# A token mixer on one core: wo's low parts go to VectorE, and VectorE's order in an iteration changes

## The chip, the cores and the metric

The kernel runs on one core of a Trainium2 chip. Its time is the device time of one execution in microseconds, the median over several executions. One core has five engines with a queue each: TensorE (PE, with its weight loads listed as PEld), VectorE (DVE), ScalarE (ACT), GpSimd (POOL) and SyncE (SP, which here only issues DMAs). An engine runs its instructions strictly in their order, so one that waits holds up all behind it.

## The reference

The input is x with 2048 tokens of 512 channels, in float32. The kernel computes

```
h  = x + attention(layernorm(x)) @ wo      # 32 heads of 16; features softmax(k@phi), softmax(-k@phi)
                                           # num = phi_q (phi_k^T v), den = phi_q (sum phi_k), o = num/den
h2 = h + mlp(layernorm(h))                 # over tokens: gelu(h^T w1 + b1) w2 + b2, 1792 hidden
```

The attention is linear: the sums over the keys (kv and zacc) are made first, and then each tile of queries is multiplied with them.

## The kernel before

Tokens are worked in 16 tiles of 128 (tile t). To keep float32 accuracy, every operand of a large product is split into a high part, which ACT makes by a copy into a rounded type, and a low part, which is the difference; a product is three matmuls (`mm3`, L61 to L63): high by high, high by low, low by high. All names ending in h and l, or in hi and lo, are such pairs.

There are four stages.

1. To about 120 us: keys and values of all tiles and the first queries, with sums of the keys' features in zacc (on POOL, L197 and L472).
2. A short passage to about 148 us (L471 to L509). The last tile's features are added to zacc by DVE (L481); PE multiplies zacc with ones, in two halves of four groups each (L486, tile pk_ps); ACT copies the result to zB, and POOL multiplies it with the queries' features (s_ez, L440, tile ez). wo is split here: `wo_hi` on ACT, `wo_lo` on POOL (L429, tile wol), two of its four parts before POOL's negate and two behind the first two ez.
3. Iterations 0 to 18 of the loop at L620, to about 276 us. In iteration `it` PE runs s_num(it-1) (L544), s_wo(it-2) (the product with wo, tile po), s_tr(it) (transposes, L526, tile tn), a query projection q_mm while there are any, and then fills: parts of the next stage's first product, `h^T w1`, for hidden groups p=0 and p=1 (tile pu).
4. The rest of the mixer: fills of the other groups, gelu, and the product with w2 (L745), with all operands split.

From L416 to the end of stage 3 the order of PE, DVE, ACT and POOL is written out by hand (`manual_schedule`): an engine executes what the Python code issues, in that order. In stage 1 and in stage 4 a scheduler sets the order.

In an iteration of stage 3 the steps that matter are these.

- s_num writes its result to the PSUM tile tn. ACT copies it to oh (L548), and DVE makes the low part ol from tn and oh (`s_ol`, L553). s_tr writes the same PSUM tile, of which there is one, so it waits until ol is made.
- `q_logits` is DVE's mx, mn and a shift (L151, L152, L144) with an ACT copy (L146, tile eq) of the other sign. That copy frees one of two PSUM slots of the query projections. The first fill of p=1 takes these slots when the projections are over, in iteration 5. POOL's `negate` (L159) then follows, and ACT's exponential.
- `q_sums` is two reductions (L214). `s_den` is DVE's chain from ez to w (L449 to L455, tile tz first), interleaved one by one with the lists above by `run`.
- `lead` puts POOL's eq by w (`s_pq`, L458) and ez (L440) for later tiles.
- `s_h(it-2)` adds the product with wo to x (L568), which frees po, of which there is one too, for the next s_wo. It stores h and then makes the mean and variance (L571 to L575, here called the statistics). `s_rstd` on POOL (L578, L579, tile r) uses these in the next iteration, `s_hn` on ACT normalizes and splits, and POOL makes the low part hs (L57).
- `fill_load` loads a piece of w1 by SP (L595, tile wraw) into one of four buffers, and splits it: ACT makes whi (L56), DVE makes wlo (L57). It stands at the end of an iteration, behind the statistics. Iterations 2, 6 and every second one after load two pieces, iterations 4 and 5 one each.

Of the kernel before, what the change touches and what calls it, by code (L numbers as in the profile page):

```python
# [11 lines left out]
AF = mybir.ActivationFunctionType  # L12
# [7 lines left out]
NT = S // P  # L20
KD = D // P
# [12 lines left out]
def block_kernel(ctx: ExitStack, tc: tile.TileContext, x, xT, wT, phic, wo, w1, b1, w2, b2,  # L34
                 kvmask, ident_in, out):
    nc = tc.nc
# [17 lines left out]
    def split(hi, lo, src, lo_engine):  # L54

        nc.scalar.activation(hi, src, AF.Copy)  # L56
        return lo_engine.tensor_sub(lo, src, hi)  # L57

    def mm3(o, ah, al, bh, bl, first, last):

        nc.tensor.matmul(o, ah, bh, start=first, stop=False)  # L61
        nc.tensor.matmul(o, ah, bl, start=False, stop=False)  # L62
        nc.tensor.matmul(o, al, bh, start=False, stop=last)  # L63
# [24 lines left out]
    zacc = wp.tile([P, NG, P], F32, name="zacc")  # L88
# [5 lines left out]
    X, XH, EQ, PK, VS, SQ, PS, W = {}, {}, {}, {}, {}, {}, {}, {}  # L94

    def load_x(t):
        raw = kk.tile([P, KD, P], F32, name="xraw", bufs=3)
        nc.sync.dma_start(raw, xT[t])
        return raw
# [36 lines left out]
    def logit_ops(src, e, pool):  # L136

        v = src.rearrange("p (j h d) -> p j h d", h=2, d=DH)
        ev = signs(e)
        mx = wk.tile([P, NPR, 2], F32, name="mx")  # L140
        mn = wk.tile([P, NPR, 2], F32, name="mn")

        def shift():
            nc.vector.tensor_sub(ev[:, :, 0], v, mx.unsqueeze(3).to_broadcast([P, NPR, 2, DH]))  # L144
            if pool:
                nc.scalar.activation(ev[:, :, 1], v, AF.Copy)  # L146
                MN.append((ev, mn))
            else:
                nc.vector.tensor_sub(ev[:, :, 1], mn.unsqueeze(3).to_broadcast([P, NPR, 2, DH]), v)

        return [lambda: nc.vector.tensor_reduce(mx, v, axis=AX.X, op=ALU.max),  # L151
                lambda: nc.vector.tensor_reduce(mn, v, axis=AX.X, op=ALU.min),  # L152
                shift]

    def negate():

        if MN:
            ev, mn = MN.pop(0)
            nc.gpsimd.tensor_sub(ev[:, :, 1], mn.unsqueeze(3).to_broadcast([P, NPR, 2, DH]), ev[:, :, 1])  # L159

    def run(*lists):

        for i in range(max(map(len, lists))):
            for ops in lists:
                if i < len(ops):
                    ops[i]()

    def exps(t, e):
        nc.scalar.activation(e, e, AF.Exp, scale=r1[:, t:t + 1])
# [39 lines left out]
    def q_sum(t):  # L209

        assert t < SUMS or t - SUMS in W, "a tile's sums would go where others are still wanted"
        SQ[t] = sums[:, t % SUMS]
        e = signs(EQ[t])
        return [lambda c=c: nc.vector.reduce_sum(SQ[t][:, :, 1 - c], e[:, :, c], axis=AX.X) for c in range(2)]  # L214
# [144 lines left out]
    def q_mm():  # L359
        if q["mm"] < NT:  # L360
            PS[q["mm"]] = proj(q["mm"], wqh, wql, ps_q, "pu")
            q["mm"] += 1

    def q_logits(lag):
        n = q["logits"]
        if n < min(NT, q["mm"] - lag + NT * (q["mm"] == NT)):
            EQ[n] = big.tile([P, NG, P], F32, name="eq", tag="big")
            q["logits"] += 1
            return logit_ops(PS[n], EQ[n], n >= len(Q_AT))
        return []  # L370
# [7 lines left out]
    def q_sums(lag):  # L378
        n = q["sum"]
        if n < min(NT, q["exp"] - lag + NT * (q["exp"] == NT)):  # L380
            q["sum"] += 1
            return q_sum(n)
        return []

    def v_kv():

        nonlocal v
        v_proj(v)
        if v % 2 == 0:
            kv(v - 2)  # L390
            kv(v - 1)
        v += 1
# [4 lines left out]
    for t in range(3, NT - 1):  # L397
        if t + 2 < NT:
            raw = load_x(t + 2)
# [22 lines left out]
    woh = w2p.tile([P, KD, D], F32R, name="woh")  # L422
    wol = w2p.tile([P, KD, D], F32R, name="wol")

    def wo_hi(j):
        nc.scalar.activation(woh[:, j], WO[j], AF.Copy)

    def wo_lo(j):
        nc.gpsimd.tensor_sub(wol[:, j], WO[j], woh[:, j])  # L429

    WO = {}
    for j in range(KD):
# [5 lines left out]
    def s_ez(t):  # L438
        EZ[t] = az.tile([P, NG, P], F32, name="ez")
        nc.gpsimd.tensor_mul(EZ[t], EQ[t], zB)  # L440
# [33 lines left out]
    k_norm(NT - 1, False)  # L474
    for j in range(KD):
        wo_hi(j)
    wo_lo(0)
    wo_lo(1)
    v_kv()
    run(q_logits(0))  # L480
    nc.vector.tensor_add(zacc, zacc, PK[NT - 1])  # L481
    negate()
    zB = big.tile([P, NG, P], F32, name="zB", tag="big")
    for g in range(2):
# [3 lines left out]
    q_exp(0)  # L488
    s_ez(0)
    s_ez(1)  # L490
    wo_lo(2)
    wo_lo(3)
    q_mm()
    v_kv()
    run(s_den(0))
# [24 lines left out]
    HN, HT, PHT, OS, PO, VE = {}, {}, {}, {}, {}, {}  # L520
# [16 lines left out]
    def s_num(t):  # L537

        pn = ps_t.tile([P, 2, 4, P], F32, name="tn")[:, :, 0:2]
        for b in range(2):  # L540
            for c in range(4):
                for r in range(2):
                    rows, cols = slice(64 * r, 64 * r + 64), slice(32 * c, 32 * c + 32)
                    nc.tensor.matmul(pn[cols, r, b, :], kvB[rows, b, cols], PHT[t][rows, 4 * b + c, :],  # L544
                                     start=True, stop=True, skip_group_check=True)
        oh = ak.tile([P, 2, 2, P], F32R, name="oh")
        ol = ak.tile([P, 2, 2, P], F32R, name="ol")
        nc.scalar.activation(oh, pn, AF.Copy)  # L548
        OS[t] = oh, ol, pn

    def s_ol(t):
        oh, ol, pn = OS[t]
        return [lambda: nc.vector.tensor_sub(ol, pn, oh)]  # L553
# [7 lines left out]
    def s_x(t):  # L561
        HT[t] = ak.tile([P, D], F32, name="h", bufs=4)
        nc.sync.dma_start(HT[t], x[t * P:(t + 1) * P, :])

    def s_h(t):

        h = HT[t]
        nc.vector.tensor_add(h, PO.pop(t), h)  # L568
        nc.sync.dma_start(out[t * P:(t + 1) * P, :], h)
        st = ak.tile([P, 6], F32, name="st2")  # L570
        nc.vector.bn_stats(st, h)  # L571
        nc.vector.bn_aggr(mv2[:, t, :], st)
        VE[t] = ak.tile([P, 2], F32, name="ve2")
        nc.vector.tensor_scalar(VE[t][:, 0:1], mv2[:, t, 1:2], 1.0 + EPS, EPS * EPS, op0=ALU.mult, op1=ALU.add)
        nc.vector.tensor_scalar_mul(VE[t][:, 1:2], mv2[:, t, 0:1], -1.0)  # L575

    def s_rstd(t):
        nc.gpsimd.tensor_tensor(r2[:, t:t + 1], VE[t][:, 0:1], mhalf[:, :1], op=ALU.pow)  # L578
        nc.gpsimd.tensor_mul(VE[t][:, 1:2], VE[t][:, 1:2], r2[:, t:t + 1])  # L579
# [7 lines left out]
    w1v = w1.rearrange("(k p) f -> p k f", p=P)  # L587
    w2v = w2.rearrange("(k p) s -> p k s", p=P)

    def stream(src, k0, n, c0, w):  # L590

        raw = wf.tile([P, n, w], F32, name="wraw")
        wh_ = wf.tile([P, n, w], F32R, name="whi")
        wl_ = wf.tile([P, n, w], F32R, name="wlo")
        nc.sync.dma_start(raw, src[:, k0:k0 + n, c0:c0 + w])  # L595
        LO.append(split(wh_, wl_, raw, nc.vector).ins)
        return wh_, wl_

    PU, WI, LO = {}, {}, []
    FN, FL = [0] * (NF // 2), [0] * (NF // 2)  # L600

    def fill_load(p):
        if FL[p] < NT:
            WI[p, FL[p]] = stream(w1v, FL[p], 2, p * 256, 256)
            FL[p] += 2

    def fill(p, pool=None):

        t = FN[p]
        FN[p] = t + 1  # L610
        if FL[p] <= t:
            fill_load(p)
        if t == 0:
            PU[p] = [pool.tile([P, D], F32, name="pu", tag="pu") for _ in range(2)]
        a, b = WI[p, t - t % 2]
        for c in range(2):
            mm3(PU[p][c], a[:, t % 2, c * P:(c + 1) * P], b[:, t % 2, c * P:(c + 1) * P],
                HN[t][:, 0], HN[t][:, 1], t == 0, t == NT - 1)

    for it in range(NT + 3):  # L620
        if 0 <= it < NT:
            s_x(it)
        if 0 <= it - 3 < NT:
            s_rstd(it - 3)
        if 0 <= it - 1 < NT:
            s_num(it - 1)
        if 0 <= it - 2 < NT:
            s_wo(it - 2)
        if it == 1:
            run(q_logits(0))  # L630
            q_mm()
        if 0 <= it < NT:
            s_tr(it)
        if it == 0:
            s_kv()
        lead(it, 1)
        den = s_den(it + 2) if it + 2 < NT else []
        run((s_ol(it - 1) if 0 <= it - 1 < NT else []) + q_logits(1) + (q_sums(0) if it > 0 else []), den)
        if it > 0:
            negate()  # L640
        if 0 <= it - 3 < NT:
            s_hn(it - 3)
        if 0 <= it - 2 < NT:
            s_h(it - 2)
        if FN[0] <= it - LAG:
            fill(0, ps_f)
        for _ in range(2):
            if q["logits"] == NT and FN[1] <= it - LAG:
                fill(1, ps_q)
        for p in range(2):  # L650
            if it >= LAG - 2 and FL[p] <= FN[p] + 1:
                fill_load(p)
    ms.close()
    a2.close()
    aq.close()
# [100 lines left out]
    for n, (sp, p) in enumerate(STEPS):  # L756
        t = 2 * sp
# [93 lines left out]
```

## Time and profile before

Three executions took 535.80, 535.86 and 536.12 us, median 535.86. The profiled execution took 535.76 us; its span, from the first instruction to the last, is 534.0 us.

| engine | busy us | share of span | instructions |
|---|---|---|---|
| PE | 522.6 | 98% | 3872 |
| DVE | 393.5 | 74% | 722 |
| POOL | 236.6 | 44% | 184 |
| ACT | 258.6 | 48% | 406 |

The shares are means over stages with different limits. In the window of 110 to 148 us POOL is busy 32.5 of 38 us, in that of 148 to 190 us DVE 40.7 of 42 us, and from 262 us on DVE 175.8 and POOL 28.1 of 272 us. The granted clock of TensorE was 0.997 of full speed on the mean. A busy PE isn't PE at its peak, since matmuls overlap; so stalls of PE are read from the starts of its matmuls, which follow each other in 0.227 us for 512 columns when nothing is waited for.

### The profile page before, as it was taken

What the parts mean: (1) busy time and instruction counts of PE and PEld (TensorE: products, weight loads), DVE (VectorE), ACT (ScalarE), POOL (GpSimd) and SP (SyncE); (2) the same over time, 40 slices, a digit from 0 to 9 for tenths busy, and PEclk for the clock granted to TensorE, in tenths of its full rate; (3) what the DMA queues carried; (4) which work ended last, traced back from release to release, by engine and by line L of the source; (5) the groups of instructions that cost most, each with busy time, mean ns of one, the idle gap of its engine ahead of it and who ended that gap; (6) DMA issues with size and microseconds to landing.
All of it is one profiled execution on the core that took longest, in us unless ns stands there. A gap on an engine that the chain in (4) does not pass through costs nothing.

```text
span 534.0 us, 9892 instructions
## 1 busy us (share of the span) xinstructions
PE 522.6 (98%) x3872; PEld 450.4 (84%) x3872; DVE 393.5 (74%) x722; ACT 258.6 (48%) x406; POOL 236.6 (44%) x184
## 2 busy tenths in 40 slices
PE   8999999998999999999999999999999999999995
PEld 7888888886876777778788888888899999999995
DVE  6993999875699989986536523835768878888774
ACT  6998844434346555544546423525443343343340
POOL 2589699878978989985435000000001101100110
PEclk9999999999999999999999999999999999999998
DMA  8534300021302233333256333533014556536631
GB/s 315 196 113 118 99 21 21 1 78 63 97 4 86 73 101 118 100 121 118 91 166 179 98 100 97 160 107 91 20 41 108 139 149 144 133 119 140 138 80 40
DMA packets 45486, 55.84 MB, mean 105 GB/s; under 512 B 3968, under 2 KB 33024, under 8 KB 45440
## 3 DMA queue, kind: packets, MB, share of 16 engines
q1 hardware_dynamic: 43136, 51.38, 30.2%
q0 software_dynamic: 2016, 3.67, 5.1%
q8 instruction: 30, 0.49, 0.4%
q10 hardware_dynamic: 288, 0.17, 0.1%
q14 instruction: 16, 0.13, 0.1%
HBM read 46.81 MB, written 8.39 MB: 103 GB/s over the span
## 4 chain that ended last, share of the span: by engine, by line
PE 91%; DVE 5%; ACT 2%; issue 1%; POOL 0%; DVEq 0%; POOLq 0%
PE py L745 26%; PE pu L61 12%; PE pu L62 12%; PE pu L63 12%; PE po L61 3%; PE pv L62 3%; PE pv L63 3%; PE pv L61 3%; PE pk_ps L61 2%; PE pk_ps L63 2%; PE pk_ps L62 2%; PE tn L526 2%; PE po L62 2%; PE po L63 2%; PE kvp L205 2%; PE tn L544 1%
## 5 line engine op out<-in xcount | busy, mean ns | idle before, releaser
L57 DVE TENSOR_TENSOR wlo<-wraw,whi 128x512 fp32r<-128x512 f32 (+1 forms) x84 | 100.3, 1204 | 69.4 <-ACT whi L56 67.9
L56 ACT ACTIVATE whi<-wraw 128x512 fp32r<-128x512 f32 (+1 forms) x84 | 81.9, 987 | 127.1 <-PE py L745 73.8
L783 POOL DMA_DIRECT2D out<-ot x14 | 12.5, 1001 | 211.3 <-DVE ot L781 211.3
L745 PE MATMUL py<-uf,whi 128*128 128x256 f32 x560 | 96.2, 283 | 0.0
L61 PE MATMUL pu<-hs,whi 128*128 128x512 f32 x224 | 87.6, 394 | 0.6 <-ACT eq L146 0.6
L62 PE MATMUL pu<-hs,whi 128*128 128x512 f32 x224 | 87.2, 389 | 0.0
L63 PE MATMUL pu<-hs,wlo 128*128 128x512 f32 x224 | 86.8, 389 | 0.0
L745 PEld LDWEIGHTS py<-uf,whi 128*128 128x128 f32 x560 | 83.3, 192 | 0.0
L745 PE MATMUL py<-uf,wlo 128*128 128x256 f32 x280 | 69.9, 283 | 0.0
L61 PEld LDWEIGHTS pu<-hs,whi 128*128 128x128 f32 x224 | 42.1, 188 | 9.5 <-ACT eq L146 1.1
L745 PEld LDWEIGHTS py<-uf,wlo 128*128 128x128 f32 x280 | 49.7, 192 | 0.0
L63 PEld LDWEIGHTS pu<-hs,wlo 128*128 128x128 f32 x224 | 42.0, 188 | 8.8
L62 PEld LDWEIGHTS pu<-hs,whi 128*128 128x128 f32 x224 | 42.1, 188 | 8.2
L528 ACT ACTIVATE pht<-tn 128x512 f32<-128x512 f32 x32 | 17.4, 596 | 49.7 <-PE tn L526 49.7
L440 POOL TENSOR_TENSOR ez<-eq,zB 128x1024 f32<-128x1024 f32 x16 | 38.4, 2406 | 0.7 <-ACT zB L487 0.7
L745 PE MATMUL py<-un,whi 128*128 128x256 f32 x224 | 38.4, 283 | 0.0
L193 POOL TENSOR_TENSOR pk<-pk,sk 128x1024 f32<-128x1024 f32 x16 | 31.1, 1944 | 9.4 <-DVE sk L192 7.6
L745 PEld LDWEIGHTS py<-un,whi 128*128 128x128 f32 x224 | 33.2, 192 | 0.1
L458 POOL TENSOR_TENSOR eq<-eq,w 128x1024 f32<-128x1024 f32 x16 | 31.1, 1942 | 3.1 <-DVE w L455 3.1
L197 POOL TENSOR_TENSOR zacc<-zacc,pk 128x1024 f32<-128x1024 f32 x13 | 31.3, 2409 | 0.6
L57 POOL TENSOR_TENSOR hs<-hn,hs 128x512 fp32r<-128x512 f32 x16 | 20.6, 1291 | 21.1 <-ACT hs L56 21.1
L61 PE MATMUL po<-woh,oh 128*128 128x512 f32 x64 | 26.6, 416 | 1.0 <-DVE h L568 1.0
(161 smaller groups left out, 1144.3 us busy)
## 6 DMA issues: line engine op xcount, KB each, us to landing
wraw<-in_w SPq DMA_DIRECT2D x112, 256.0 KB, 2.8
xraw<-in_xT SPq DMA_DIRECT2D x16, 256.0 KB, 3.1
xh<-in_x SPq DMA_DIRECT2D x16, 256.0 KB, 2.7
h<-in_x SPq DMA_DIRECT2D x16, 256.0 KB, 2.9
out<-h SPq DMA_DIRECT2D x16, 256.0 KB, 2.2
out<-ot POOLq DMA_DIRECT2D x14, 256.0 KB, 4.8
wraw<-in_wT SPq DMA_DIRECT2D x12, 256.0 KB, 4.9
wo<-in_wo SPq DMA_DIRECT2D x4, 256.0 KB, 3.8
```

Of the source, the lines that this page charges most:

```text
L56: nc.scalar.activation(hi, src, AF.Copy)
L57: return lo_engine.tensor_sub(lo, src, hi)
L61: nc.tensor.matmul(o, ah, bh, start=first, stop=False)
L62: nc.tensor.matmul(o, ah, bl, start=False, stop=False)
L63: nc.tensor.matmul(o, al, bh, start=False, stop=last)
L193: nc.gpsimd.tensor_mul(heads(PK[t]), heads(PK[t]), sk.unsqueeze(2).to_broadcast([P, 2 * H, DH]))
L197: nc.gpsimd.tensor_add(zacc, zacc, PK[t])
L440: nc.gpsimd.tensor_mul(EZ[t], EQ[t], zB)
L458: nc.gpsimd.tensor_mul(heads(EQ[t]), heads(EQ[t]), W[t].rearrange("p g c h -> p (g c h)").unsqueeze(2).to_broadcast([P, 2 * H, DH]))
L528: nc.scalar.activation(PHT[t][:, half * 4:half * 4 + 4, :], ptr[:, half], AF.Copy)
L745: nc.tensor.matmul(o, a[x], b[:, y], start=start and i == 0, stop=stop and i == 2, skip_group_check=True)
L783: nc.gpsimd.dma_start(out[(t + i) * P:(t + i + 1) * P, :], flat(ot[:, i]), accum_op=ALU.add)
```

## The change

There are two parts. In stage 2, the four low parts of wo move from POOL to DVE and stand behind zacc, which is added in two halves of four groups. In stage 3, the add of h is taken out of the end of DVE's iteration and put in fourth place of the list that `run` executes, behind ol, tz and the first of mx or the sums; there it is followed by `flush`, which makes the low parts of the w1 pieces that an earlier `fill_load` put on the list LATER. The statistics stay at the end as `s_stats`. In stage 4 `fill` calls `flush` itself right behind `fill_load`. ACT's and PE's order in stages 2 and 3 is as before, and POOL only loses the four low parts.

```diff
     def wo_lo(j):
-        nc.gpsimd.tensor_sub(wol[:, j], WO[j], woh[:, j])
+        nc.vector.tensor_sub(wol[:, j], WO[j], woh[:, j])
...
     for j in range(KD):
         wo_hi(j)
-    wo_lo(0)
-    wo_lo(1)
     v_kv()
     run(q_logits(0))
-    nc.vector.tensor_add(zacc, zacc, PK[NT - 1])
+    for g in range(2):
+        nc.vector.tensor_add(zacc[:, 4 * g:4 * g + 4, :], zacc[:, 4 * g:4 * g + 4, :], PK[NT - 1][:, 4 * g:4 * g + 4, :])
+    for j in range(KD):
+        wo_lo(j)
     negate()
...
     s_ez(1)
-    wo_lo(2)
-    wo_lo(3)
     q_mm()
...
+    LATER = []
+
+    def flush():
+        while LATER:
+            wl_, raw, wh_ = LATER.pop(0)
+            LO.append(nc.vector.tensor_sub(wl_, raw, wh_).ins)
...
-        LO.append(split(wh_, wl_, raw, nc.vector).ins)
+        nc.scalar.activation(wh_, raw, AF.Copy)
+        LATER.append((wl_, raw, wh_))
...
             fill_load(p)
+            flush()
...
-        run((s_ol(it - 1) if 0 <= it - 1 < NT else []) + q_logits(1) + (q_sums(0) if it > 0 else []), den)
+        ops = turns((s_ol(it - 1) if 0 <= it - 1 < NT else []) + q_logits(1) + (q_sums(0) if it > 0 else []), den)
+
+        ops[3:3] = ([lambda: s_h(it - 2)] if 0 <= it - 2 < NT else []) + [flush]
+        run(ops)
...
         if 0 <= it - 2 < NT:
-            s_h(it - 2)
+            s_stats(it - 2)
```

`turns` is the interleaving that `run` did before, as a list; `run` now executes one list. `s_stats` is the second half of the old `s_h`.

More of the change, by code (lines that the diff above doesn't have):

```diff
@@ L56, in split @@
         nc.scalar.activation(hi, src, AF.Copy)
-        return lo_engine.tensor_sub(lo, src, hi)
+        lo_engine.tensor_sub(lo, src, hi)
     def mm3(o, ah, al, bh, bl, first, last):
@@ L159, in negate, with turns @@
             nc.gpsimd.tensor_sub(ev[:, :, 1], mn.unsqueeze(3).to_broadcast([P, NPR, 2, DH]), ev[:, :, 1])
+    def turns(*lists):
+        return [ops[i] for i in range(max(map(len, lists))) for ops in lists if i < len(ops)]
     def run(*lists):
[L163 to L166, printed above, removed]
+        for op in turns(*lists):
+            op()
     def exps(t, e):
@@ L569, in s_h, with s_stats @@
         nc.sync.dma_start(out[t * P:(t + 1) * P, :], h)
+    def s_stats(t):
+        h = HT[t]
         st = ak.tile([P, 6], F32, name="st2")
@@ L652, in block_kernel @@
                 fill_load(p)
+    flush()
     ms.close()
```

## The prediction

> **What bounds the kernel now.** I read the page first (busy shares), then the table of waits of TensorE (PE), the windows of the stage, and the timeline of VectorE (DVE), ScalarE (ACT) and GpSimd (POOL) there. The last column of the table is the longest wait in us.
>
> ```profile
> span 534.0 us, 9892 instructions
> PE 522.6 (98%) x3872; PEld 450.4 (84%) x3872; DVE 393.5 (74%) x722; ACT 258.6 (48%) x406; POOL 236.6 (44%) x184
> ...
> PE pk_ps L486 <- DVE zacc L481: 1.7, 1, 1.7
> PE po L61 <- DVE h L568: 1.0, 1, 1.0
> PE pu L61 <- ACT eq L146: 0.6, 1, 0.6
> PE tn L526 <- DVE ol L553: 0.5, 1, 0.5
> ...
> 148.00:190.00 42.00, 40.27 (x367) 31.07 (x366) 40.71 (x90) 23.36 (x39) 36.08 (x27) 1.00 0.19 60
> ```
>
> PE sets the time: busy 98%, and after 262 us its matmuls follow each other without a gap. What an edit of order can still win are the four waits between 124 and 201 us. In starts of matmuls they are 1.85 us (zacc), 1.3, 0.8 and 0.7 us. The window's columns are length, then busy time of PE, PEld, DVE, ACT, POOL: from 148 to 190 us DVE is busy 40.7 of 42 us and POOL 36.1. So there PE has almost no cover: what makes DVE longer by a microsecond reaches PE soon.
>
> ```profile
> 123.96 3.48 POOL L429 TENSOR_TENSOR wol<-wo,woh 128x512 fp32r<-128x512 f32 x2
> ...
> 124.03 2.28 DVE L481 TENSOR_TENSOR zacc<-zacc,pk 128x1024 f32<-128x1024 f32 x1
> ...
> 188.21 1.29 POOL L57 TENSOR_TENSOR hs<-hn,hs 128x512 fp32r<-128x512 f32 x1 [0.30 <-ACT hs L56]
> ...
> 188.79 1.27 DVE L57 TENSOR_TENSOR wlo<-wraw,whi 128x512 fp32r<-128x512 f32 x1
> ...
> 291.66 1.72 POOL L692 TENSOR_TENSOR tt<-u,tt 128x256 f32<-128x256 f32 x1
> ...
> 291.56 1.23 DVE L57 TENSOR_TENSOR un<-u,un 128x1024 fp32r<-128x1024 f32 x1 [0.58 <-ACT un L56]
> 292.70 1.23 DVE L57 TENSOR_TENSOR wlo<-wraw,whi 128x512 fp32r<-128x512 f32 x1
> ...
> 298.11 0.69 DVE L57 TENSOR_TENSOR wlo<-wraw,whi 128x512 fp32r<-128x512 f32 x1 [2.03 <-ACT whi L56]
> ...
> 173.64 1.94 POOL L458 TENSOR_TENSOR eq<-eq,w 128x1024 f32<-128x1024 f32 x1
> 175.53 2.41 POOL L440 TENSOR_TENSOR ez<-eq,zB 128x1024 f32<-128x1024 f32 x1
> ```
>
> Columns: start, duration, engine, line. A wlo takes 0.69 us alone (298.11), and 1.27 when it starts inside POOL's hs: it ends at 190.06, 0.56 after hs ends. Both read two SBUF tiles. At 291.56 un (1.21 alone) runs, POOL's L692 waits for it and then goes, and the wlo behind un waits for L692: a DVE and a POOL instruction of this kind take turns, whole.
>
> The Trainium skill, SBUF — State Buffer, section "Who interferes with whom", says a VectorE instruction with two SBUF inputs and a GpSimd instruction that reads SBUF exclude each other for the whole of the one that issued first. The rows agree as far as they go (at most 1.29 us of POOL); none shows a wlo against the 2.41 us ez.
>
> **Part 1, wo's low parts and zacc.** POOL loses four wol (1.28 to 1.30 each alone), DVE gains four (0.69 each). With no wol at 123.96, POOL is idle from 124.00 (end of L193) until ACT's eq copy of 125.74 ends. So zacc's halves run alone: half of a 1.2 us instruction, 0.6 to 0.7 each, done at 124.7 and 125.3 instead of 126.31. PE's matmul on the first half starts 0.15 later, as now, at 124.85 for 126.46; it lasts 0.9, so the second half is there. Gain 1.6 us, all on PE. The four wol on DVE lie in its idle 5.25 us before 131.57; one may meet POOL's negate or ez(0) and be done by 131; their reader is s_wo at 156 us. POOL's next ez starts 1.6 earlier. PE has no other wait until 163, and DVE idles 4.1 us before 144.4, so the 1.6 reaches iteration 2. Bounds 0 and 1.85.
>
> **Part 2, the order on DVE.** T is the start of s_num of an iteration. Rows of PE: s_tr at T+3.45 if ol is done, next s_num at T+7.15 (155.42, 158.87, 162.57); a fill adds 1.36. Rows of DVE, an iteration without wlo: 7.32 (165.44 to 172.76) while there are logits, 6.23 (199.55 to 205.78) after. New order: ol, tz, mx or sum, h, then wlo, so wlo begins 3.04 us after ol begins (0.60+1.12+0.60+0.72), 3.16 later on. POOL starts when the statistics end: r 0.55, ve, then pq (L458) at +0.88, ez (L440) at +2.78 until +5.2. DVE begins the next ol just when the statistics end, where DVE is the late one. So wlo, which now comes behind the statistics and meets only hs or r, falls into ez. It waits about 2.1 us, then takes 0.6 (the pitch of two in a row); a second wlo 0.6 more, or 1.25 more yet where hs is queued and takes its turn. What is queued behind: the logits' shift, the sums, w, the statistics and the next ol. Of h, the add, its store on SP and its load are as many as before; the store goes out some 3 us earlier. SP's loads of wraw wait for wlo about 3 us longer; whi needs them an iteration or more later. Cover: four buffers.
>
> Worked on the new axis (1.6 earlier), iteration by iteration:
> - Iteration 2 (T 153.8): no wlo. h at 157.5 just finds s_wo done (157.4). DVE ends at 162.6, as now less 1.6.
> - Iteration 3 (T 160.9): ol 162.6, two wlo ready at 165.64; ez runs 165.35 to 167.76. They end at 168.9 and the iteration at 173.2. Iteration 4 has T 168.1, its s_tr could go at 171.5, and ol is read at 174.05: PE stands 2.5 us. Here PE now loses 1.4 (0.3 at 166, 1.1 at 171.7). Term +1.1.
> - Iteration 5 (T 179.1): oh lets ol start at 180.9; one wlo ready at 183.94, ez(8) from 183.75: done 186.74. The shift ends 188.2, ACT's eq copy 188.9. The fill that takes tile 15's PSUM slot could go at T+6.39 = 185.5: it waits 3.4, now 0.8. Term +2.6. If wlo got in ahead of ez (the two are 0.2 apart), shift 186.0, copy 186.65, wait 1.2: term +0.4. I take +2.6.
> - Iteration 6: wlo no longer waits for whi (0.84 at 197.66), and ol is in time for s_tr (now 0.7 late). Term -0.8.
> - Iterations 7, 9, 11 have two wlo each: 6.23+1.2+2.1 to 3.3 = 9.5 to 10.8, and with the even one 15.8 to 17.0 against PE's 14.30. The first starts with ol at T+2.5 (oh is late behind whi), and s_tr of iteration 8 stands 1.7; those of 10 and 12 stand 1.4 to 2.7 and 1.5 to 2.8. Terms +1.7, +2.0, +2.1.
> - From 12 on there are no sums (4.95 us per iteration), from 13 no ez: nothing more. Behind 262 us PE has its whole queue of fills: nothing.
>
> Sum: -1.6 +1.1 +2.6 -0.8 +1.7 +2.0 +2.1 = +7.1 us. The profiled execution took 535.76 (span 534.0 and 1.8 around it), 0.1 under the median of 535.86, so 542.9 us. Ends with this lock: +0.4 for 2.6 and the low ends, +3.8; the high ends, +8.5.
>
> A price no row has is the wait behind ez. Low end: the 0.6 us that wlo waited behind hs. Then a flush is 1.2 or 1.8 us and the pair of iterations 14.26, inside 14.30: terms -1.6, -0.4, +1.0, -0.8 = -1.8. I take the whole of ez, since each contended row waited to the end of the POOL instruction, however long. By the Trainium skill's rule the wait is the whole of ez too, which gives the +7.1; the 0.6 alone gives the -1.8.
>
> **Rivals.**
> - No wait behind ez: wlo costs 1.2 for two, 0.6 for one. Then iteration 3 ends at 171.1 and s_tr of 4 stands 0.4; iteration 5's wait is 1.0; the rest none. -1.6 -1.0 +0.2 -0.8 = -3.2: 532.6 us, with the low end above 534.0. This is the other sign. For it: the four waits of PE do hang on DVE's order, and h comes 3.3 us earlier. Against: the rows of contention. It decides at a wait of 0.6 us per flush of two, where the pair of iterations equals 14.30.
> - The lock holds, but wlo slips in ahead of ez where it is one, and ahead of hs: +3.8 to +5.5, 539.5 to 541.3 us. For: 0.2 us between the two in iteration 5. Against: where two are to go, ez lies between them or ahead of them either way.
>
> **How the numbers follow.** Lock, whole ez: 0.54 (541.3 to 544.5). Lock, luckier order: 0.23 (537 to 541.3). Between 534.8 and 536.9, within 0.2%, about what can be told from no change: 0.05. Faster: 0.18. Left out of 535.0 to 544.5 are the faster case and 0.02 above. The likeliest case's own range is 541.3 to 544.5.
>
> **What would show it.** zacc in two of 0.6 to 0.7 us and PE's wait there under 0.3 (right for part 1). In the timeline of 160 to 245 us, wlo of 2 us and more beside ez, longer DVE iterations where there is a wlo, and PE waiting at tn L526 for ol in iterations 4, 8, 10, 12 and at the first fill of p=1 for eq. The wait po for h should be gone. Wrong: wlo at 0.69 inside ez, or POOL so late that pq and not ez meets it.

## The result and the profile after

The changed kernel takes 538.76 us (median of six executions, 538.23 to 540.83) against 535.99 us for the kernel before (six, 535.80 to 536.47): a ratio of 1.0054, with a 95% interval of 1.0042 to 1.0066. It is 2.8 us slower, where 7.1 us slower was forecast. The profiled execution took 538.99 us.

The page and PE's waits in the whole span, of the changed kernel (time in all, times, longest, in us):

```profile
span 537.2 us, 9882 instructions
...
PE 523.6 (97%) x3872; PEld 450.8 (84%) x3872; DVE 399.4 (74%) x727; ACT 258.7 (48%) x406; POOL 227.7 (42%) x180
...
PE tn L526 <- DVE ol L553: 5.3, 4, 2.1
PE pk_ps L287 <- DVE mhalf L52: 1.1, 1, 1.1
PE pk_ps L123 <- ACT wkh L279: 0.8, 1, 0.8
PE pu L61 <- ACT eq L146: 0.7, 1, 0.7
```

The waits for zacc (1.7) and for h (1.0) are gone. The two of pk_ps were there before and lie in stage 1. What is new is the first row: the transposes s_tr now wait four times for ol, 5.3 us in all, where they waited once for 0.5. DVE's busy time has grown by 5.9 us. POOL's has fallen by 8.9. The larger parts of that are the four wol that it lost, 6.0, and r (L578 before, L581 now), which had met wlo, from 13.4 to 8.9; ez and hs, which meet wlo now, have grown by 3.2.

The windows (length; busy time of PE, PEld, DVE, ACT, POOL; granted clock, DMA share, GB/s), first of the changed kernel:

```profile
148.00:190.00 42.00, 39.22 (x341) 30.56 (x334) 39.78 (x87) 22.83 (x37) 35.35 (x27) 1.00 0.20 64
190.00:262.00 72.00, 68.77 (x597) 53.76 (x597) 60.45 (x126) 34.59 (x58) 53.67 (x45) 1.00 0.30 100
262.00:534.00 272.00, 269.79 (x1773) 247.09 (x1771) 176.07 (x305) 108.76 (x143) 26.38 (x32) 1.00 0.42 112
```

and of the kernel before, the middle one:

```profile
190.00:262.00 72.00, 71.47 (x641) 56.21 (x639) 59.17 (x131) 36.83 (x62) 55.14 (x46) 1.00 0.35 113
```

PE loses 2.7 us between 190 and 262 us, where it had been busy for 71.5 of 72: 44 fewer matmuls are done there, of which 32 are the short ones of one s_num. Behind 262 us it is full again, and what was lost comes at the end.

The timeline of the changed kernel at the places that the prediction named (start, duration, engine and line; in brackets idle time before it and who ended that):

```profile
124.77 1.30 DVE L481 TENSOR_TENSOR zacc<-zacc,pk 128x512 f32<-128x512 f32 x2
125.98 5.57 DVE L430 TENSOR_TENSOR wol<-wo,woh 128x512 fp32r<-128x512 f32 x4
...
165.97 2.40 POOL L441 TENSOR_TENSOR ez<-eq,zB 128x1024 f32<-128x1024 f32 x1
166.27 3.25 DVE L598 TENSOR_TENSOR wlo<-wraw,whi 128x512 fp32r<-128x512 f32 x2
...
174.55 1.06 PE L526 MATMUL tn<-ident,eq 128*128 128x128 f32 x8 [2.05 <-DVE ol L553]
...
184.12 0.70 DVE L598 TENSOR_TENSOR wlo<-wraw,whi 128x512 fp32r<-128x512 f32 x1
184.23 2.84 POOL L441 TENSOR_TENSOR ez<-eq,zB 128x1024 f32<-128x1024 f32 x1
...
216.70 3.52 DVE L598 TENSOR_TENSOR wlo<-wraw,whi 128x512 fp32r<-128x512 f32 x2
216.82 2.85 POOL L441 TENSOR_TENSOR ez<-eq,zB 128x1024 f32<-128x1024 f32 x1
...
219.63 1.74 POOL L57 TENSOR_TENSOR hs<-hn,hs 128x512 fp32r<-128x512 f32 x1
```

There are three cases in it. At 166.27 ez is already running: the two wlo take 3.25 us, where the two at 164.24 us of the kernel before took 1.27 together, and PE's transposes at 174.55 come after 2.05 us of waiting. At 184.12 the single wlo begins 0.11 us before ez: it takes 0.70, and it is ez that is longer (2.84 instead of 2.40). At 216.70 the first of two wlo begins 0.12 us before ez; the second waits through all of it (0.72 and 2.88 us, one by one), and then hs waits for that one (1.74 instead of 1.29). The four wol at 125.98 take 5.57 us and not 2.4, as they meet negate and the first ez on POOL. That costs PE nothing: it waits for nothing from there to 174.55.

The group of all wlo from 160 to 246 us (count, busy us, mean ns, idle before), changed kernel:

```profile
L598 DVE TENSOR_TENSOR wlo<-wraw,whi 128x512 fp32r<-128x512 f32 x10 | 15.7, 1605 | 0.0
```

and before:

```profile
L57 DVE TENSOR_TENSOR wlo<-wraw,whi 128x512 fp32r<-128x512 f32 x12 | 11.4, 982 | 2.0 <-ACT whi L56 2.0
```

### The profile page after: what moved, and what is told of

Read it like the earlier page. It is cut to its first block, busy times and chain, and to the rows that moved or that the text cites. A ratio compares the mean times of both kernels' runs of the same rounds, so it can differ in the third digit from the quotient of the medians.

```text
span 537.2 us, 9882 instructions
## 1 busy us (share of the span) xinstructions
PE 523.6 (97%) x3872; PEld 450.8 (84%) x3872; DVE 399.4 (74%) x727; ACT 258.7 (48%) x406; POOL 227.7 (42%) x180
## 4 chain that ended last, share of the span: by engine, by line
PE 85%; DVE 11%; ACT 2%; issue 1%; POOL 0%; DVEq 0%; POOLq 0%; ACTq 0%
PE py L761 26%; PE pu L61 11%; PE pu L62 11%; PE pu L63 11%; PE pv L62 3%; PE pv L63 3%; PE pv L61 3%; PE pk_ps L61 2%; DVE wlo L598 2%; PE pk_ps L62 2%; PE pk_ps L63 2%; PE tn L526 2%; PE po L61 2%; PE kvp L206 2%; DVE smq L215 1%; PE po L62 1%
## 5 line engine op out<-in xcount | busy, mean ns | idle before, releaser
L56 ACT ACTIVATE whi<-wraw 128x1792 fp32r<-128x1792 f32 x28 | 47.7, 1705 | 77.9 <-PE py L761 67.2
L598 DVE TENSOR_TENSOR wlo<-wraw,whi 128x512 fp32r<-128x512 f32 x56 | 47.6, 862 | 44.9 <-ACT whi L606 44.6
L57 DVE TENSOR_TENSOR wlo<-wraw,whi 128x1792 fp32r<-128x1792 f32 x28 | 56.6, 2023 | 18.5 <-ACT whi L56 18.4
L606 ACT ACTIVATE whi<-wraw 128x512 fp32r<-128x512 f32 x56 | 34.4, 628 | 48.3 <-PE pu L62 44.1
L441 POOL TENSOR_TENSOR ez<-eq,zB 128x1024 f32<-128x1024 f32 x16 | 40.5, 2534 | 0.1
```

The costliest lines, as they stand in the source:

```text
L598: LO.append(nc.vector.tensor_sub(wl_, raw, wh_).ins)
L606: nc.scalar.activation(wh_, raw, AF.Copy)
```

## The experiments

The theory is the forecast's: the new place of wlo meets ez, and an instruction of DVE and one of POOL that contend take turns, whole. Rivals are that the new order costs by itself (h early, statistics late), and that part 1, by which PE reaches the loop earlier, takes slack away from it.

**1. Part 1 alone**, on the kernel before.

```diff
-        nc.gpsimd.tensor_sub(wol[:, j], WO[j], woh[:, j])
+        nc.vector.tensor_sub(wol[:, j], WO[j], woh[:, j])
...
-    nc.vector.tensor_add(zacc, zacc, PK[NT - 1])
+    for g in range(2):
+        nc.vector.tensor_add(zacc[:, 4 * g:4 * g + 4, :], zacc[:, 4 * g:4 * g + 4, :], PK[NT - 1][:, 4 * g:4 * g + 4, :])
+    for j in range(KD):
+        wo_lo(j)
...
```

> Part 1 alone: wo's low parts on VectorE behind zacc in halves, the loop of before. Theory (PE's wait for zacc goes, and the loop follows 1.6 us earlier): 1.4 to 1.7 us under before, about 534.3 us, PE's wait before pk_ps under 0.3 us, the waits at po, eq and tn as in before. Rival (GpSimd's early lead or VectorE's four extra instructions change the loop): the loop's waits differ and the time is within 0.5 us of before or above it.

Measured: 534.6 us (nine executions, 534.0 to 535.09) against 536.05 (thirteen), ratio 0.9972, interval 0.9962 to 0.9981. PE's waits from 124 to 205 us:

```profile
PE po L61 <- DVE h L567: 1.0, 1, 1.0
PE pu L61 <- ACT eq L146: 0.6, 1, 0.6
PE tn L525 <- DVE ol L552: 0.5, 1, 0.5
```

The wait for zacc is gone and the three of the loop are what they were. Part 1 gains 1.45 us and has no part in the loss.

**2. Part 2 alone**: the new order of the loop on the stage 2 of before.

```diff
-        run((s_ol(it - 1) if 0 <= it - 1 < NT else []) + q_logits(1) + (q_sums(0) if it > 0 else []), den)
+        ops = turns((s_ol(it - 1) if 0 <= it - 1 < NT else []) + q_logits(1) + (q_sums(0) if it > 0 else []), den)
+        ops[3:3] = ([lambda: s_h(it - 2)] if 0 <= it - 2 < NT else []) + [flush]
+        run(ops)
...
-            s_h(it - 2)
+            s_stats(it - 2)
...
```

> Part 2 alone: VectorE's new order in the loop, wo's low parts on GpSimd and zacc whole as before. Theory (the two parts add; the loop alone costs about 4.3 us by the waits of the changed kernel): 3.8 to 4.6 us over before, about 540.2 us, PE's waits at tn for ol in iterations 4, 8, 10 and 12. Rival (the loop's loss hangs on PE arriving early from part 1): under 3 us over before.

Measured: 542.32 us (four executions, 540.39 to 542.9), ratio 1.0113, interval 1.0097 to 1.0129. PE's waits:

```profile
PE tn L527 <- DVE ol L554: 5.3, 4, 2.1
PE pk_ps L487 <- DVE zacc L482: 1.7, 1, 1.7
PE pu L61 <- ACT eq L146: 1.5, 1, 1.5
```

The row of tn is that of the changed kernel, so the loss belongs to part 2. But 6.3 us is more than the 3.8 to 4.6 that were expected, and more than the parts' sum allows: 6.3 less 1.45 is 4.8, and both together cost 2.8. The profiled execution shows two things that make up the other 2. PE's matmuls, just behind the wait for ol in iteration 4, came at half their pace:

```profile
175.87 1.42 PE L527 MATMUL tn<-ident,eq 128*128 128x128 f32 x8 [2.06 <-DVE ol L554]
...
177.94 0.63 PE L63 MATMUL pu<-wqh,xs 128*128 128x512 f32 x1
178.37 0.63 PE L61 MATMUL pu<-wqh,xs 128*128 128x512 f32 x1
...
180.19 0.39 PE L63 MATMUL pu<-wqh,xs 128*128 128x512 f32 x1
180.42 0.39 PE L61 MATMUL pu<-wqh,xs 128*128 128x512 f32 x1
```

They start 0.43 us apart at 178 and 0.23 apart at 180. The windows of the same execution give the clock (third number from the end):

```profile
176.40:179.80 3.40, 3.40 (x12) 2.82 (x11) 3.40 (x9) 2.42 (x4) 3.40 (x2) 0.50 0.20 77
180.00:184.00 4.00, 4.00 (x48) 2.97 (x47) 2.26 (x9) 2.55 (x5) 3.92 (x6) 1.00 0.18 66
```

Half the clock for 3.4 us costs 1.6 us: iteration 4 lasts 12.36 us here and 10.77 in the changed kernel. The second thing follows from the first. PE came to iteration 5 later by that, and with it ol and wlo, but POOL did not, so that wlo began behind ez:

```profile
185.51 2.39 POOL L441 TENSOR_TENSOR ez<-eq,zB 128x1024 f32<-128x1024 f32 x1
...
186.89 1.57 DVE L599 TENSOR_TENSOR wlo<-wraw,whi 128x512 fp32r<-128x512 f32 x1
```

This ez comes 1.28 us later than in the changed kernel, but this wlo 2.77. The fill waited 1.5 us for it, against 0.7, and iteration 5 lasts 10.28 us against 9.56. The three executions of 542.1 us and more show a mean clock of 0.994 or 0.995, the one of 540.39 us shows 0.997; it is the one that comes out near the expected 540.2. More of this in the last section.

**3. wlo at the end again, h still early**, on the changed kernel.

```diff
-        ops[3:3] = ([lambda: s_h(it - 2)] if 0 <= it - 2 < NT else []) + [flush]
+        ops[3:3] = ([lambda: s_h(it - 2)] if 0 <= it - 2 < NT else [])
...
                 fill_load(p)
+                flush()
```

> The changed kernel, but w1's low parts are made at the end of an iteration again, right behind their high parts and behind the statistics; h stays third behind ol. Theory (the loss comes from wlo meeting GpSimd's ez, not from h): no wlo over 1.4 us in the loop, the waits at tn in iterations 8, 10 and 12 go, the 0.7 of before at iteration 7 comes back, the wait at iteration 4 falls to 0.5 or less; 2.0 to 3.0 us under before, about 533.4 us. Rival (h in the middle, with the statistics apart, is what makes VectorE late): 537 us or more.

Measured: 533.63 us (five executions, 533.07 to 533.83), ratio 0.9955, interval 0.9943 to 0.9968. The group of wlo from 160 to 246 us, and PE's waits there:

```profile
L598 DVE TENSOR_TENSOR wlo<-wraw,whi 128x512 fp32r<-128x512 f32 x12 | 11.7, 1004 | 2.3 <-ACT whi L606 2.2
```

```profile
PE pu L61 <- ACT eq L146: 1.0, 1, 1.0
PE tn L526 <- DVE ol L553: 0.5, 1, 0.5
```

The mean of wlo is back at 1.0 us from 1.6, and the four waits of tn are one of 0.5. Moving wlo alone turns 538.76 into 533.63, so its place costs the changed kernel 5.1 us. Against experiment 1 the early h gains 1.0 us: PE loses 1.2 less in iterations 3 and 4, where it waited for h and ol, and 0.3 more in iteration 5. The new order by itself is no loss, and that rival falls.

**4. The changed kernel without ez** for tiles 3 to 15.

```diff
-            s_ez(it + 3)
+            EZ[it + 3] = EZ[1 + it % 2]
```

> The changed kernel without the product ez of GpSimd for tiles 3 to 15; the denominators of these tiles are made from the ez of tile 1 or 2, so they aren't the reference's. VectorE's order is that of the changed kernel. Theory (the lock on ez): every wlo in the loop takes 0.6 to 0.7 us or meets only the product L459, the waits at tn in iterations 8, 10 and 12 go and that in iteration 4 falls under 1 us; 532 to 534 us. Rival (the place of wlo in VectorE's order costs by itself, by what is queued behind it): the waits at tn stay at 1 us or more, 537 to 539 us.

Measured: 532.9 us (five executions, 532.24 to 533.56), ratio 0.9944, interval 0.9931 to 0.9958. The group of wlo from 160 to 246 us, and the only wait of PE from 124 to 205 us:

```profile
L598 DVE TENSOR_TENSOR wlo<-wraw,whi 128x512 fp32r<-128x512 f32 x12 | 7.8, 682 | 0.0
```

```profile
PE pu L61 <- ACT eq L146: 0.7, 1, 0.7
```

With the place of wlo as in the changed kernel and ez taken away, every wlo takes 0.68 us, and the waits for ol are gone. So ez is what wlo waits for. The Trainium skill, SBUF — State Buffer, section "Who interferes with whom", has it that the two engines share a port pair under a lock held for the whole instruction; the 3.25 us beside an ez of 2.40, and 0.68 without one, agree with that.

**5. wlo 0.7 us later in iteration 5 alone**, on the changed kernel, to see what its 0.11 us ahead of ez were worth.

```diff
-        ops[3:3] = ([lambda: s_h(it - 2)] if 0 <= it - 2 < NT else []) + [flush]
+        ops[3:3] = [lambda: s_h(it - 2)] if 0 <= it - 2 < NT else []
+        at = 6 if it == 5 else 4 if 0 <= it - 2 < NT else 3
+        ops[at:at] = [flush]
```

> The changed kernel, but in iteration 5 alone wlo stands two instructions later (behind mn), some 0.7 us, so that it comes after the start of ez instead of 0.1 us ahead of it. Theory (the predicted 2.6 us of iteration 5 failed by that 0.1 us alone): wlo takes 2 us or more, the fill that waits for ACT's copy of tile 15 stands 2.3 to 2.8 us instead of 0.9, 1.4 to 1.9 us over the changed kernel, 540.2 to 540.7 us, and up to 1.7 more where TensorE's clock drops behind the longer idle time. Rival (that fill's wait is set by ACT's order, not by VectorE): within 0.3 us of the changed kernel.

Measured: 540.39 us (four executions, 540.18 to 541.61), ratio 1.0085, interval 1.0071 to 1.0098. The timeline and PE's wait for the fill:

```profile
184.26 2.39 POOL L441 TENSOR_TENSOR ez<-eq,zB 128x1024 f32<-128x1024 f32 x1
184.86 2.34 DVE L598 TENSOR_TENSOR wlo<-wraw,whi 128x512 fp32r<-128x512 f32 x1
```

```profile
PE pu L61 <- ACT eq L146: 2.4, 1, 2.4
```

Now ez keeps its 2.39 us and wlo takes 2.34. The wait for eq goes from 0.7 to 2.4 and the time from 538.76 to 540.39. The mechanism that the forecast had for iteration 5 exists; in the changed kernel it was missed by 0.11 us.

**6. wlo one iteration later, ahead of the statistics**, on the kernel of experiment 3 (iteration 5's at the end), to find a better place.

```diff
         run(ops)
+        flush()
...
                 fill_load(p)
-                flush()
+                if it == 5:
+                    flush()
```

> As the run with wlo at the end, but the low parts of an iteration's w1 pieces are made one iteration later, between w and the statistics, when GpSimd's ez has ended; those of iteration 5 right behind their high parts. Theory (what is left there of VectorE's lateness is the wait for whi and hs): no wlo over 1.4 us, the 0.7 us at iteration 7 goes, 0.5 to 1.0 us under the run with wlo at the end, about 532.9 us. Rival (the statistics, 1.2 us later, hold GpSimd up and with it the ez that follows): no gain or a loss against that run.

Measured: 534.56 us (eight executions, 534.46 to 535.03), ratio 0.9973, interval 0.9963 to 0.9983: 0.9 us slower than experiment 3, not faster. The timeline, and PE's wait:

```profile
168.19 1.06 POOL L159 TENSOR_TENSOR eq<-mn,eq 128x512 f32<-128x512 f32 x1 [0.63 <-PE pu L63]
168.66 2.84 DVE L598 TENSOR_TENSOR wlo<-wraw,whi 128x512 fp32r<-128x512 f32 x2
169.55 1.41 POOL L57 TENSOR_TENSOR hs<-hn,hs 128x512 fp32r<-128x512 f32 x1 [0.30 <-ACT hs L56]
```

```profile
PE tn L526 <- DVE ol L553: 1.6, 1, 1.6
```

This place meets negate and then hs. The first wlo waits for negate. Then hs, which came at 169.55 while that wlo was held up or running, goes ahead of the second, which comes at 169.7. PE lost 1.87 us in iteration 4, against 0.08 in experiment 3. The step from s_num to ol is 4.42 us there and 2.62 in experiment 3. So the loss that the rival named came, but by DVE's own delay and not by a later ez. In iteration 5 PE lost 0.81 us against 1.17: the wlo of the piece that iteration 4 loads no longer stands ahead of DVE's work there.

**7. ACT's eq copy ahead of the exponential in iteration 5**, on the kernel of experiment 3, whose wait for eq (1.0) is longer than that of before (0.6).

```diff
-        lead(it, 1)
+        lead(it, 1, it != 5)
...
         run(ops)
+        if it == 5:
+            q_exp(0)
```

> As the run with wlo at the end, but in iteration 5 ACT copies tile 15's logits before the exponential of tile 14. Theory (the fill of iteration 5 waits there on ACT's exponential, not on VectorE): the 1.2 us wait for eq in iteration 5 falls to 0.4 or less, 0.6 to 1.0 us under that run, about 532.8 us. Rival (VectorE's shift comes last): the wait stays above 0.8 us.

Measured: 533.31 us (five executions, 533.11 to 533.83), ratio 0.9951, interval 0.9937 to 0.9964; that is no change from 533.63 that can be told. The copy in the timeline:

```profile
183.86 0.60 ACT L146 ACTIVATE eq<-pu 128x512 f32<-128x512 f32 x1 [1.26 <-DVE eq L144]
```

ACT now idles 1.26 us for DVE's shift (L144, done at 183.83). So the rival was right: DVE was last there, not ACT.

**8. Experiments 6 and 7 together.**

> Both together: wlo one iteration later ahead of the statistics, and in iteration 5 the copy ahead of the exponential. Theory: the two gains add, 1.2 to 1.9 us under the run with wlo at the end, about 532.1 us, with no wait of TensorE over 0.5 us after the start. Rival: one uncovers the other's wait, and less than 1.0 us is gained.

Measured: 534.15 us (five executions, 533.98 to 534.96), ratio 0.9966, interval 0.9954 to 0.9979. The wait in iteration 5 falls to 0.25 us, so both were needed: with DVE earlier ACT's order counts. But the loss in iteration 4 (1.87 us) stays and outweighs it: 0.5 us over experiment 3, where 1.2 to 1.9 under it were expected.

**9. Each wlo where nothing meets it to harm**: experiment 7, with the pieces that iterations 4 and 6 load made one iteration later, ahead of the statistics, and all others at the end.

```diff
         if it == 5:
             q_exp(0)
+        if it in (5, 7):
+            flush()
...
                 fill_load(p)
-                flush()
+                if it not in (4, 6):
+                    flush()
```

> As the run with wlo at the end and iteration 5's copy ahead of its exponential, but only the pieces loaded in iterations 4 and 6 have their low parts one iteration later, ahead of the statistics. Theory (each place is taken where the earlier runs showed no wait: 0.1 at iteration 4, 0.3 at iteration 5, 0 at iteration 7): 1.2 to 1.7 us under the run with wlo at the end, about 532.1 us. Rival (VectorE's lateness only moves on to the next iteration): 533 us or more.

Measured: 532.23 us (five executions, 531.63 to 532.75) against 536.25 (nine), ratio 0.9925, interval 0.9911 to 0.9938. PE's waits in the whole span:

```profile
PE pk_ps L287 <- DVE mhalf L52: 1.1, 1, 1.1
PE pk_ps L123 <- ACT wkh L279: 0.8, 1, 0.8
```

None is left behind stage 1. It beats both kernels, by 4.0 us and by 6.5 us of medians. It keeps part 1 and the early h of the change, and puts back or delays the low parts.

## Why the prediction was right and where it was wrong

The direction and the mechanism were right: slower, by the wait of wlo behind ez, with PE waiting at tn in iterations 4, 8, 10 and 12. The fifth place, the fill of iteration 5, was wrong, and with it the size. The measured 538.76 us is in the range of the luckier order (537 to 541.3), which had 0.23, and not in the likeliest one. What PE lost or won can be read from the starts of s_num, iteration by iteration, against the time an iteration takes without a wait:

| term | forecast | measured |
|---|---|---|
| zacc | -1.6 | -1.57 |
| iterations 3 and 4 | +1.1 | +0.86 |
| iteration 5 | +2.6 | +0.11 |
| whi (DVE in 6, s_tr in 7) | -0.8 | -0.73 |
| iteration 8 | +1.7 | +1.68 |
| iteration 10 | +2.0 | +1.09 |
| iteration 12 | +2.1 | +1.14 |
| sum | +7.1 | +2.58 |

The spans of the two profiled executions differ by 3.2 us; the other 0.7 is there at 120 us already, ahead of all that was changed. Executions of the same code differ by as much there: the last product kvp before 120 us begins at 118.74 us in the changed kernel, and at 118.01 and 117.96 in experiments 4 and 6. The medians differ by 2.8.

- **Iteration 5 is the step that failed.** The forecast saw that wlo and ez would be 0.2 us apart, with ez first, and took +2.6 over the +0.4 that it gave for wlo first. In the changed kernel wlo was 0.11 us ahead. Moved onto that trace's axis (0.73 later, as at 120 us), the forecast had wlo at 184.67 and ez at 184.48; they came at 184.12 and 184.23, the first 0.55 us early and the second 0.25. Most of it is ol, which came 0.44 us early. Experiment 5 shows the other side of it: 1.6 us more for 0.7 us of delay. With positions off by that much, the choice between the two orders was close to a coin toss, and the sum should not have hung on one side of it. This one term is 2.5 of the 4.5 us that the sum was too high.
- **Iterations 10 and 12 were sized too high.** The forecast allowed a pair of DVE iterations 15.8 to 17.0 us and took the middle, for a second wlo that waits for hs as well. From ol to ol the pair 9 and 10 took 9.42 and 5.98, together 15.40 (213.77, 223.19 and 229.17 us below), which is 1.10 over PE's 14.30, just what PE lost. The odd iteration came out at the low end (9.5), and the even one 0.25 under the 6.23 taken from before. Since the first wlo got in ahead of ez, the second was already waiting when ez ended, and hs, which POOL can only offer after ez, came behind it. The +1.25 needed hs to be offered before the second wlo was: experiment 6 shows that case, at 169.55. These two terms are 1.9 of the 4.5 us.

```profile
213.77 0.69 DVE L553 TENSOR_TENSOR ol<-tn,oh 128x512 fp32r<-128x512 f32 x1
...
223.19 0.68 DVE L553 TENSOR_TENSOR ol<-tn,oh 128x512 fp32r<-128x512 f32 x1
...
229.17 0.69 DVE L553 TENSOR_TENSOR ol<-tn,oh 128x512 fp32r<-128x512 f32 x1
```

- **zacc** went as worked out: two halves in 1.30 us, and PE starts 1.57 us earlier. Experiment 1 gives 1.45 us for the whole part. Of the four wol not one but two met POOL's work (1.56 and 2.89 us), at no cost to PE.
- **The wait for h** is gone, as forecast; with it went part of PE's wait in iteration 4, 1.2 us by experiment 3 against experiment 1, of which 0.3 came back in iteration 5.
- **The price that no row had**, the wait behind ez, is the whole of ez where ez is first. Experiment 4 rules out the 0.6 us of the low end.
- **The rivals.** The one without a wait behind ez said 532.6 us; experiment 4 brings that about by taking ez away, and comes to 532.9. That the two are so close doesn't prove the sum, since without ez POOL also has 2.4 us less to do in each iteration. The one in which wlo slips in ahead of ez and hs gave 539.5 to 541.3: it is what happened in iterations 5, 9 and 11, while in 3, 6 and 7 ez was first. The time is 0.7 us below the low end of that range, of which 0.3 each for iterations 10 and 12 are the shorter pair above. (By its own terms the low end adds up to +3.7, not +3.8.) What was held against it, that ez lies between two wlo anyway, is true and leaves out that hs is then the one to wait.

## What to carry to other kernels

Before an instruction of VectorE with two SBUF inputs is moved, find what GpSimd runs at the new place: beside ez a wlo of 0.69 us took up to 2.9, and the place alone cost 5.1 us. When two contenders fall within some tenths of a microsecond of each other, work out both orders and give each its share, because either may come: the changed kernel had wlo first in iteration 5, and the same order of instructions had ez first in experiment 2, where PE was late by its clock. A change that loses can hold two that win: here the early h and part 1 were worth 1.0 and 1.45 us, and the move of wlo that came with them hid both.

## What the runs showed of the hardware

TensorE's clock fell to 0.5 for 3.4 us behind a wait of 2.06 us, in the profiled execution of experiment 2 (176.4 to 179.8 us); the mean clocks of two more of its four executions suggest the same. The changed kernel waited 2.05 us at the same place in its profiled execution, and there the clock stayed at 1.00, as it did in that of experiment 5 behind waits of 2.05 and 2.37 us:

```profile
174.60:178.00 3.40, 3.40 (x20) 2.94 (x21) 3.40 (x7) 2.12 (x3) 3.32 (x4) 1.00 0.12 46
```

One of its other executions has a mean clock of 0.995 and took 540.83 us, 2 us above the median; whether it is the same can't be seen without its profile. The Trainium skill, TensorE: Matmul & The Clock Gate, section "Part 1: The HAM clock gate (the "warmup" mystery)", puts the halving behind an idle window of about 3.4 us that runs free of the kernel. The 3.4 us at half speed and the difference between two executions with equal waits fit that; the length of the wait alone doesn't, as 2.06 us were enough. Eight transposes follow it, to 176.94 us, and no run here shows whether the gate counts them as idle time. So a wait of 2 us can cost another 1.6, in some executions and not in others, and more where a late PE turns the order of two contenders, as in experiment 2.

A second point is the order of turns, read from these rows only. Whichever of two waiting instructions was offered first goes first: in the changed kernel the wlo that had waited since 217.3 us went ahead of the hs at 219.63, and in experiment 6 the hs of 169.55 us ahead of the wlo of 169.7.
